# Retention followed by a snake-activated projection: half of the diagonal score and value products left out in three of eight batches

## The chip, the cores and the metric

The kernel runs on one core of a Trainium2 chip. The metric is device time in microseconds for one execution. Three executions of the kernel before took 309.53, 309.72 and 309.93 us; the median is 309.72 us.

The core has a matrix engine (TensorE, PE in the profile, with its weight loads as PEld), VectorE (DVE), ScalarE (ACT), GpSimd (POOL) and SyncE (SP). SyncE computes nothing here: it issues nearly all DMAs, one after the other, in the order in which the program names them.

## The reference

Two steps follow one another. The first is a causal retention over 8 batches, 8 heads, 576 tokens and 64 features a head:

```
scores = q @ k^T / sqrt(64)                          # per batch and head
ret    = scores * gamma[h] ** (i - j)   for i >= j, else 0
x      = ret @ v                                     # heads side by side: 4608 tokens x 512
```

The second is two matrix products with a snake function between them:

```
h   = x @ w_in                                       # 512 -> 2048
g   = h + sin(alpha * h) ** 2 / (alpha + 1e-9)
out = g @ w_out                                      # 2048 -> 512
```

## The kernel before, in words

**The retention in chunks.** A batch's first 512 tokens are four chunks of 128 tokens; the last 64 tokens of every batch are treated apart, two batches together (the class `Ends`, tensors `ks`, `qs`, `vs`). Since gamma ** (i - j) is a product of a factor of the query and a factor of the key, the factors (`cn`) are multiplied in when the inputs are cast to 16 bits. Within a chunk, scores are masked by i >= j; what earlier chunks contribute goes through a state of 64 x 64 per head (`outer` makes it from keys and values, `chain` on GpSimd carries it along, `add_states` multiplies it by the queries).

**Loads.** `load(b, nm, p)` brings half p (256 tokens, two chunks) of the keys, queries or values of batch b into a buffer `raw` with one DMA of 512 KB from SyncE's queue. A chunk lies on 64 partitions: partition 64 g + i holds, for chunk g of the half, the tokens 2 i and 2 i + 1 of the chunk, so a run in memory is two tokens, 512 B. The letter r tells the two apart. There are six such buffers.

**Cast and transpose.** `cast` multiplies by the factors and writes 16 bits (line 156 for keys and queries, line 99 on GpSimd for values); from batch 5 on GpSimd does all of them. `crossed` turns keys and queries with a DMA transpose from SyncE (line 179).

**Attention on TensorE.** All of it works on 64 x 64 quadrants of the array, four matmuls side by side.
- `scores(p, y)` (line 328): 16 matmuls, each with 64 keys of one r and one head against the 128 queries of the chunk. Four calls a batch.
- `masked` (line 339): VectorE multiplies 128 x 1024 scores by the mask and writes `ret`.
- `values(p, same)` (line 368): 16 matmuls of 64 values against 128 columns of `ret`. [...] 

**The order of the work.** It is written out by hand. Up to block 2 every step has a line of its own. From block n = 3 on a loop runs over blocks of 512 tokens: for each of 16 units u it runs `project` (line 503, four matmuls of 512 columns), `sine` on ScalarE (line 511), `square` on ScalarE or VectorE (lines 520 and 522), `product` on VectorE (line 527), and `gemm2` of the block before (line 546, four matmuls of 512 columns). After every fourth unit `finish` copies a result out of PSUM and SyncE stores it (line 539, two DMAs). The results of `project` rotate over three banks (`h`); stores go through four buffers (`osb`).

Attention is woven into this loop: in block n, batch n + 1 has its scores in units 3 and 8 and its values in unit 12, and batch n + 2 is loaded, cast (units 3 to 8, in the order k0, v0, k1, v1, q0, q1), transposed (units 13 and 15) and has its `outer` (unit 12). So batches 5, 6 and 7 are attended in blocks 4, 5 and 6 and loaded one to two blocks earlier. In unit 12, the two `values(..., False)` come first, then `outer` of the next batch, then the two `values(..., True)` with `add_states`.

Of the kernel before, what the change touches and what calls it, by code (L numbers as in the profile page):

```python
# [10 lines left out]
F32 = mybir.dt.float32  # L11
# [6 lines left out]
def kernel(  # L18
# [12 lines left out]


    nc = tc.nc

# [12 lines left out]
    cn_np = np.zeros((P, 52), dtype=np.float64)  # L47
# [16 lines left out]
    ident = const.tile([P, P], F16, tag="ident", bufs=1)  # L64
    mask = const.tile([P, 5 * 64], F16, tag="mask", bufs=1)
    cn = const.tile([P, 52], F32, tag="cn", bufs=1)
    fac = {"k": cn[:, 0:16], "q": cn[:, 16:32]}
    fac_s = {"k": cn[:, 32:40], "q": cn[:, 40:48]}
# [36 lines left out]
    def load(b, nm, p):  # L105
        if p < 2:
            t_ = work.tile([P, H, 2 * D], F32, tag="raw", bufs=6, name=nm + "32")
            nc.sync.dma_start(  # L108
                t_, src[nm][b, :, 256 * p : 256 * p + 256, :].rearrange("h (i r) d -> i h (r d)", r=2)
            )  # L110
        else:
            if b % 2 == 0:
                raw[b, nm, 2] = work.tile([P, H, D], F32, tag="raws", bufs=3, name=nm + "s32")
            t_ = raw[b - b % 2, nm, 2]
            nc.sync.dma_start(t_[halves(b % 2)], src[nm][b, :, 512:576, :].rearrange("h i d -> i h d"))
        raw[b, nm, p] = t_
# [3 lines left out]
    def cast(b, nm, p, eng, ys=(0, 1)):  # L120
# [32 lines left out]
        else:  # L153
# [4 lines left out]
                t_.rearrange("p (t a) x -> p t a x", t=2)[:, :, a0:a1].rearrange("p t a (r d) -> p t (a r) d", r=2),  # L158
                fac[nm]
                .rearrange("p (t x) -> p t x", t=2)[:, :, 2 * a0 : 2 * a1]  # L160
# [67 lines left out]
    class Attention:  # L228
        def __init__(self, b):
            self.b = b  # L230
            self.both = {}
# [87 lines left out]
        def scores(self, p, y, tag):  # L319
            kT, qT = T[self.b, "k", p], T[self.b, "q", p]  # L320
            sc = psum.tile([P, 2, 512], F32, tag=tag, bufs=1, name="sc")
            for z in range(2):
                a = 2 * y + z
                for r in range(2):
                    for g in range(2):
                        for t in range(2):
                            c = 256 * z + 128 * r
                            matmul(  # L328
                                sc[halves(g), t, c : c + 128],
                                kT[halves(t), 2 * a + r, halves(g)],  # L330
                                qT[halves(t), 2 * a : 2 * a + 2, halves(g)],
                                start=(z == 0 and r == 0), stop=True, skip_group_check=True,
# [3 lines left out]
        def masked(self, p, y):  # L336
            sc = self.sc.pop((p, y))
            ret = work.tile([P, 2, 512], F16, tag="ret", bufs=4, name="ret")
            nc.vector.tensor_tensor(  # L339
                ret.rearrange("p t (z x) -> p (t z) x", z=2),  # L340
                sc.rearrange("p t (z x) -> p (t z) x", z=2),
                mask[:, 0:256].unsqueeze(1).to_broadcast([P, 4, 256]),
                MULT,
# [3 lines left out]
        def values(self, p, same, *tags, relay=None):  # L347
# [13 lines left out]
            for x in range(2):  # L361
                for r in range(2):
                    for e in range(2):
                        for g in range(2):
# [3 lines left out]
                            made.append(matmul(  # L368
                                o[t][halves(e), c : c + 128],
                                v16[halves(g), 4 * t + 2 * x + e, r, :],  # L370
                                self.ret[p, x][halves(g), t, m : m + 128],
                                start=(not same and x == 0 and r == 0), stop=False, skip_group_check=True,
# [203 lines left out]
    def make_constants():  # L576

        ge = mybir.AluOpType.is_ge
        nc.gpsimd.memset(ident, 0.0)
# [5 lines left out]
        for g in range(2):  # L585
# [7 lines left out]
                out=m, in_=m, compare_op=ge, fill=0.0, base=0, pattern=[[1, 64]], channel_multiplier=-1,  # L593
            )

    with tc.manual_schedule():
# [481 lines left out]
        at[4].to_state(2, G_)  # L1078
        crossed(4, 0, "q")

        h, m = cycle(("h2", "h0", "h1")), cycle(("m0", "m1"))
        ON_A = (4, 5, 6, 8, 9)
        for n in range(3, NBLK):
# [54 lines left out]
            for u in range(16):  # L1138
# [63 lines left out]
```

## Time and profile before

| what | before |
|---|---|
| median of three executions | 309.72 us |
| profiled execution, its own time | 310.26 us |
| span in the profile (first to last instruction) | 308.5 us |
| mean granted TensorE clock | 0.989 |
| TensorE busy | 295.6 us (96%) |
| VectorE, ScalarE, GpSimd busy | 206.7, 181.0, 135.2 us |
| HBM read, written | 36.74 MB, 9.44 MB |

A row of a timeline begins with the start in microseconds from the start of the span and the duration of the row; then come engine, line of the kernel, operation, what is written and read, shape and count. In square brackets stands how long the engine was idle before and what ended that. Matmuls are pipelined and their ends are modelled, so the time that a group of matmuls takes is best read from its start to the start of the next group. In a row by stretch (A:B), each engine's busy time and number of instructions follow the length of the stretch, and at the end stand the granted clock, the mean busy share of the 16 DMA engines (over 1 where packets overlap) and GB/s. In a row of groups, the busy time and the mean of one instruction in ns stand after the first bar, and the engine's idle time before them, with what ended it, after the second.

### The profile page before, as it was taken

To read this page: it belongs to the slowest core of one execution; us is meant where nothing else is said; L and a number is where in the kernel's file an instruction comes from. 1 tells how busy PE (TensorE), PEld (TensorE's weight loads), DVE (VectorE), ACT (ScalarE), POOL (GpSimd) and SP (SyncE) were. 2 spreads that over 40 slices of the span, in tenths; PEclk is the share of its full clock that TensorE was granted. 3 is DMA by queue.
4 is the path that set the end of the run, shared out by engine and by line. 5 is a ranking of instruction groups with operands and counts; after the bars stand their busy time and mean duration, and the time that the engine had idled before them with its cause. 6 is when DMAs were issued, how large, how long until landed. Compare 5 with 4: busy or idle time off the path is not lost.

```text
span 308.5 us, 7866 instructions
## 1 busy us (share of the span) xinstructions
PE 295.6 (96%) x3257; PEld 151.0 (49%) x3257; DVE 206.7 (67%) x298; ACT 181.0 (59%) x286; POOL 135.2 (44%) x150
## 2 busy tenths in 40 slices
PE   6679899999999999999999999999999999999995
PEld 5555456555444544454445444544454454444443
DVE  1686899899669798657765776666666746555600
ACT  1348864675444857674768476857674456555411
POOL 4684772288759589469266926650030000000000
PEclk9599999999999999999999999999999999999999
DMA  7999999999998899879898999763431111111232
GB/s 206 292 228 216 225 249 266 218 262 276 204 213 233 125 231 260 171 111 218 219 261 123 235 213 259 116 130 75 102 70 36 34 36 36 35 34 37 46 89 69
DMA packets 102676, 49.83 MB, mean 162 GB/s; under 512 B 44640, under 2 KB 98160, under 8 KB 102640
## 3 DMA queue, kind: packets, MB, share of 16 engines
q1 hardware_dynamic: 98048, 44.97, 67.0%
q0 software_dynamic: 4224, 4.19, 8.0%
q8 instruction: 25, 0.41, 0.6%
q10 hardware_dynamic: 368, 0.17, 0.2%
q14 instruction: 11, 0.09, 0.1%
HBM read 36.74 MB, written 9.44 MB: 150 GB/s over the span
## 4 chain that ended last, share of the span: by engine, by line
PE 75%; DMA 12%; POOL 5%; issue 3%; ACT 2%; SPq 1%; DVE 0%; POOLq 0%; DVEq 0%; ACTq 0%
PE ops L546 36%; PE hps L503 32%; DMA v<-in_v_dram 5%; DMA q<-in_q_dram 4%; DMA qT<-q 3%; PE o L368 2%; PE sc L328 2%; POOL k L156 1%; POOL q L156 1%; PE kv L269 1%; SPq L108 1%; ACT s_t L511 1%; POOL kvs L311 1%; POOL s L303 1%; PE o L390 1%
## 5 line engine op out<-in xcount | busy, mean ns | idle before, releaser
L546 PE MATMUL ops<-w_out,gT 128*128 128x512 f16 (+2 forms) x592 | 142.5, 374 | 0.3 <-ACT kvs L97 0.2
L527 DVE SCALAR_TENSOR_TENSOR gT<-ss_t,inva,hps 128x512 f16<-128x512 f16 x144 | 106.3, 746 | 52.8 <-ACT ss_t L520 46.0
L511 ACT ACTIVATE s_t<-hps,alpha_t 128x512 f16<-128x512 f32 x144 | 97.4, 687 | 70.7 <-PE hps L503 69.1
L503 PE MATMUL hps<-xT,w_in 128*128 128x512 f16 (+1 forms) x544 | 126.6, 367 | 0.4 <-DMA w_in<-in_moe_w_in_dram 0.2
L503 PEld LDWEIGHTS <-w_in 128*128 128x128 f16 x608 | 58.6, 98 | 64.6 <-DMA w_in<-in_moe_w_in_dram 0.7
L546 PEld LDWEIGHTS <-gT 128*128 128x128 f16 x592 | 56.2, 98 | 64.5 <-issue 0.8
L522 DVE TENSOR_TENSOR ss_t<-s_t 128x512 f16<-128x512 f16 x72 | 40.5, 564 | 17.9 <-ACT s_t L511 17.5
L339 DVE TENSOR_TENSOR ret<-sc,mask 128x1024 f16<-128x1024 f32 x32 | 38.4, 1219 | 3.1 <-PE sc L328 3.1
L520 ACT ACTIVATE ss_t<-s_t 128x512 f16<-128x512 f16 x62 | 38.8, 631 | 0.9
L156 POOL TENSOR_TENSOR q<-q,cn 128x1024 f16<-128x1024 f32 (+1 forms) x16 | 27.4, 1722 | 13.7 <-DMA q<-in_q_dram 13.6
L97 ACT COPY osb<-ops 128x512 f32<-128x512 f32 (+1 forms) x34 | 19.7, 582 | 21.9 <-PE ops L546 20.3
L156 POOL TENSOR_TENSOR k<-k,cn 128x1024 f16<-128x1024 f32 (+1 forms) x13 | 21.7, 1671 | 20.8 <-DMA k<-in_k_dram 16.1
L140 POOL TENSOR_TENSOR ks<-ks,cn 128x512 f16<-128x512 f32 x4 | 4.2, 1044 | 34.2 <-PE o L368 34.2
L311 POOL TENSOR_TENSOR kvs<-s,kvs 128x256 f32<-128x256 f32 x22 | 16.4, 747 | 2.6 <-ACT kvs L97 0.9
L97 ACT CAST xT<-o 128x1024 f16<-128x1024 f32 (+1 forms) x14 | 13.2, 957 | 6.1 <-PE o L390 6.1
L503 PE MATMUL hps<-xS,w_in 128*128 128x512 f16 x64 | 16.4, 379 | 0.0
L522 POOL TENSOR_TENSOR ss_t<-s_t 128x512 f16<-128x512 f16 x10 | 10.8, 1086 | 11.4 <-ACT s_t L511 11.4
L310 POOL TENSOR_TENSOR s<-kvs,cn 128x256 f32<-128x256 f32 x22 | 13.6, 620 | 0.6 <-ACT kvs L97 0.4
L99 POOL CAST v<-v 128x1024 f16<-128x1024 f32 (+1 forms) x10 | 10.2, 1030 | 8.3 <-DMA v<-in_v_dram 8.3
L303 POOL TENSOR_TENSOR s<-kvs,cn 128x256 f16<-128x256 f32 x19 | 12.7, 674 | 1.1 <-issue 0.4
L368 PE MATMUL o<-ret,v 64*64 64x128 f16 x512 | 11.5, 219 | 0.8 <-DVE ret L339 0.4
L328 PE MATMUL sc<-qT,kT 64*64 64x128 f16 x512 | 11.5, 225 | 0.6 <-DMA qT<-q 0.4
(58 smaller groups left out, 139.2 us busy)
## 6 DMA issues: line engine op xcount, KB each, us to landing
out_dram<-osb SPq DMA_DIRECT2D x70, 128.0 KB, 2.5
k<-in_k_dram SPq DMA_DIRECT2D x16, 512.0 KB, 6.8
q<-in_q_dram SPq DMA_DIRECT2D x16, 512.0 KB, 6.9
v<-in_v_dram SPq DMA_DIRECT2D x16, 512.0 KB, 6.3
w_in<-in_moe_w_in_dram POOLq DMA_DIRECT2D x4, 512.0 KB, 12.5
w_out<-in_moe_w_out_dram POOLq DMA_DIRECT2D x4, 512.0 KB, 11.4
ks<-in_k_dram SPq DMA_DIRECT2D x8, 128.0 KB, 4.5
qs<-in_q_dram SPq DMA_DIRECT2D x8, 128.0 KB, 3.6
```

What stands on the lines that cost most here:

```text
L97: eng.copy(d_, s_)
L156: eng.tensor_tensor(dst[:, a0:a1].rearrange("p a r t d -> p t (a r) d"), t_.rearrange("p (t a) x -> p t a x", t=2)[:, :, a0:a1].rearrange( ...
L311: nc.gpsimd.tensor_tensor(self.kvs[:, c], s32, self.kvs[:, c], ADD)
L328: matmul(sc[halves(g), t, c : c + 128], kT[halves(t), 2 * a + r, halves(g)], qT[halves(t), 2 * a : 2 * a + 2, halves(g)], start=(z == 0 an ...
L339: nc.vector.tensor_tensor(ret.rearrange("p t (z x) -> p (t z) x", z=2), sc.rearrange("p t (z x) -> p (t z) x", z=2), mask[:, 0:256].unsque ...
L368: made.append(matmul(o[t][halves(e), c : c + 128], v16[halves(g), 4 * t + 2 * x + e, r, :], self.ret[p, x][halves(g), t, m : m + 128], sta ...
L503: matmul(hps_of[n, fc][0][:, cols], w_in16[:, a, fc * P : (fc + 1) * P], xs[n][:, a, cols], start=(a == 0 and part != 1), stop=(a == KT - ...
L511: nc.scalar.activation(s_t, hps, mybir.ActivationFunctionType.Sin, bias=0.0, scale=alpha_t[:, fc : fc + 1],)
L520: nc.scalar.activation(ss_t, s_t, mybir.ActivationFunctionType.Square)
L522: eng.tensor_tensor(ss_t, s_t, s_t, MULT)
L527: nc.vector.scalar_tensor_tensor(gT[n][:, fc, :], ss_t, inva[:, fc : fc + 1], hps, MULT, ADD)
L546: matmul(ops[n, c, cols.start][:, cols], gT[n][:, fk, c * P : (c + 1) * P], w_out16[:, fk, cols], start=(fk == 0), stop=(fk == FC - 1), sk ...
```

## The change

For batches 5, 6 and 7 (`HALVED = 5`) keys and values are laid out differently; queries stay as they are.

- Partition 64 g + i now holds, for r = 0, token i of the first 64 tokens of chunk g, and for r = 1, token i of the second 64. A run in memory is one token, 256 B. One load of keys or values becomes four DMAs of 128 KB, each of 64 partitions; twelve loads become 48 DMAs.
- Keys with r = 1 are later than every query of the first half of the chunk. So for r = 1 `scores` multiplies only the queries i from 32 to 63 of each kind (the second half of the chunk): 64 columns instead of 128. `values` multiplies 64 columns of `ret` for r = 1 likewise, and adds into the second halves of the output rows.
- `masked` handles 192 of 256 columns a head, 768 instead of 1024 elements a partition, with a mask of its own; `make_constants` makes it with four more selects on GpSimd and a longer memset. The keys' factors have 16 columns of their own in `cn`.
- All six loads of batch 5 are placed earlier by up to three units: three of them ahead of the loop, the other three in units 0 to 2 of block 3, ahead of that block's first output stores.
- In blocks 4 to 6, the square of unit 6 goes from ScalarE to VectorE, that of unit 10 the other way.

The number of matmuls and weight loads does not change, nor does their order.

```diff
+    HALVED = 5
...
+            cn_np[:, 52 + 2 * h + r] = gamma[h] ** (64 - (64 * r + ii))
...
     def load(b, nm, p):
-        if p < 2:
+        if p < 2 and b >= HALVED and nm != "q":
+            t_ = work.tile([P, H, 2 * D], F32, tag="raw", bufs=6, name=nm + "32")
+            for g in range(2):
+                for r in range(2):
+                    s0 = 256 * p + 128 * g + 64 * r
+                    nc.sync.dma_start(
+                        t_[halves(g), :, r * D : r * D + D], src[nm][b, :, s0 : s0 + 64, :].rearrange("h i d -> i h d")
+                    )
+        elif p < 2:
...
                 for r in range(2):
+                    i0, n = (32, 64) if self.halved and r else (0, 128)
...
                             matmul(
-                                sc[halves(g), t, c : c + 128],
+                                sc[halves(g), t, c : c + n],
                                 kT[halves(t), 2 * a + r, halves(g)],
-                                qT[halves(t), 2 * a : 2 * a + 2, halves(g)],
+                                qT[halves(t), 2 * a : 2 * a + 2, 64 * g + i0 : 64 * g + 64],
...
+            n, m0 = (192, 320) if self.halved else (256, 0)
             nc.vector.tensor_tensor(
-                ret.rearrange("p t (z x) -> p (t z) x", z=2),
-                sc.rearrange("p t (z x) -> p (t z) x", z=2),
-                mask[:, 0:256].unsqueeze(1).to_broadcast([P, 4, 256]),
+                ret.rearrange("p t (z x) -> p (t z) x", z=2)[:, :, 0:n],
+                sc.rearrange("p t (z x) -> p (t z) x", z=2)[:, :, 0:n],
+                mask[:, m0 : m0 + n].unsqueeze(1).to_broadcast([P, 4, n]),
...
                             made.append(matmul(
-                                o[t][halves(e), c : c + 128],
+                                o[t][halves(e), c : c + 128].rearrange("p (r i) -> p r i", r=2)[:, :, i0:64],
                                 v16[halves(g), 4 * t + 2 * x + e, r, :],
-                                self.ret[p, x][halves(g), t, m : m + 128],
+                                self.ret[p, x][halves(g), t, m : m + n],
...
+            for c0, n in ((320, 64), (448, 32)):
+                m = mask[halves(g), c0 : c0 + 2 * n].rearrange("p (r i) -> p r i", r=2)
+                nc.gpsimd.affine_select(
+                    out=m, in_=m, compare_op=ge, fill=0.0,
+                    base=0, pattern=[[1, 2], [2, n]], channel_multiplier=-1,
+                )
...
         crossed(4, 0, "q")
+        load(5, "k", 0)
+        load(5, "v", 0)
+        load(5, "k", 1)
...
-                if n == 3:
-                    at_unit(i, lambda nm=nm, p=p: load(5, nm, int(p)))
-                elif n < 6 and i > 2:
+                if n < 6 and i > 2:
                     at_unit(i - 3, lambda nm=nm, p=p: load(n + 2, nm, int(p)))
...
-                    square(n, u, A_ if A and u in ON_A else V)
+                    square(n, u, A_ if A and u in (ON_A if n < 4 else (4, 5, 8, 9, 10)) else V)
```

More of the change, by code (lines that the diff above doesn't have):

```diff
@@ L46 @@
     hi, ii = np.divmod(np.arange(P), 64)
[L47 removed]
+    cn_np = np.zeros((P, 68), dtype=np.float64)
     for h in range(H):
@@ L64 @@
     ident = const.tile([P, P], F16, tag="ident", bufs=1)
-    mask = const.tile([P, 5 * 64], F16, tag="mask", bufs=1)
-    cn = const.tile([P, 52], F32, tag="cn", bufs=1)
-    fac = {"k": cn[:, 0:16], "q": cn[:, 16:32]}
+    mask = const.tile([P, 8 * 64], F16, tag="mask", bufs=1)
+    cn = const.tile([P, 68], F32, tag="cn", bufs=1)
+    fac = {"k": cn[:, 0:16], "q": cn[:, 16:32], "halved k": cn[:, 52:68]}
     fac_s = {"k": cn[:, 32:40], "q": cn[:, 40:48]}
@@ L158, in cast @@
                 t_.rearrange("p (t a) x -> p t a x", t=2)[:, :, a0:a1].rearrange("p t a (r d) -> p t (a r) d", r=2),
-                fac[nm]
+                fac["halved k" if nm == "k" and b >= HALVED else nm]
                 .rearrange("p (t x) -> p t x", t=2)[:, :, 2 * a0 : 2 * a1]
@@ L230, in __init__ @@
             self.b = b
+            self.halved = b >= HALVED
             self.both = {}
@@ L362, in values @@
                 for r in range(2):
+                    i0, n = (32, 64) if self.halved and r else (0, 128)
                     for e in range(2):
```

## The prediction

> **What bounds the kernel now.** I read the page first (busy shares and the forty slices), then the busy time of each engine by stretch, then the timelines of TensorE, GpSimd and SyncE around the attention of batches 5 to 7, and last the waits of GpSimd.
>
> ```profile
> PE 295.6 (96%) x3257; PEld 151.0 (49%) x3257; DVE 206.7 (67%) x298; ACT 181.0 (59%) x286; POOL 135.2 (44%) x150
> PE   6679899999999999999999999999999999999995
> DMA  7999999999998899879898999763431111111232
> ```
>
> TensorE is busy all the time from the sixth slice on. The DMA engines are nearly as full until about 200 us.
>
> ```profile
> core 0: us, PE busy (x) PEld busy (x) DVE busy (x) ACT busy (x) POOL busy (x), PEclk, DMA share, GB/s
> 133.00:164.00 31.00, 31.00 (x360) 15.08 (x348) 21.18 (x28) 20.91 (x34) 18.99 (x19) 1.00 0.98 205
> 164.00:195.00 31.00, 31.00 (x360) 15.05 (x351) 21.22 (x28) 20.91 (x34) 19.00 (x19) 1.00 0.94 205
> 195.00:226.00 31.00, 31.00 (x348) 14.98 (x337) 20.01 (x28) 20.92 (x34) 9.29 (x13) 1.00 0.54 103
> ```
>
> These three stretches are about the blocks n = 4, 5, 6, in which batches 5, 6, 7 are attended. TensorE has no idle time in any, and the granted clock is 1.00; VectorE, ScalarE and GpSimd have 10 us or more. So a shorter matmul here comes off the end one for one, as long as nothing starts to make TensorE wait; and work taken from another engine is worth nothing.
>
> **What the matmuls give.** Per batch there are four score groups of 16 matmuls and four value groups of 16. In each, half (r = 1) go from 128 columns to 64: 32 + 32 a batch, 192 in all. The number of matmuls and weight loads stays.
>
> ```profile
> 146.40 0.64 PE L328 MATMUL sc<-qT,kT 64*64 64x128 f16 x32
> 146.97 1.04 PE L546 MATMUL ops<-w_out,gT 128*128 128x512 f16 x4
> ...
> 163.29 0.64 PE L368 MATMUL o<-ret,v 64*64 64x128 f16 x32
> 163.76 0.72 PE L269 MATMUL kv<-v,k 64*64 64x64 f16 x64
> 164.30 0.41 PE L368 MATMUL o<-ret,v 64*64 64x128 f16 x16
> 164.52 0.30 PE L390 MATMUL o<-qT,s 64*64 64x128 f16 x8
> 164.64 0.47 PE L368 MATMUL o<-ret,v 64*64 64x128 f16 x16
> 164.92 0.41 PE L390 MATMUL o<-qT,s 64*64 64x128 f16 x16
> ```
>
> From start to start, 32 score matmuls take 0.57 us (17.8 ns each), the value matmuls 0.47 for 32 and 0.22 and 0.28 for 16 (14.7, 13.8, 17.5 ns), and 64 outer-product matmuls of 64 columns take 0.54 us (8.4 ns each), weight loads included. The quadrants of the array work four at a time. How much does a halved one save? At the least 13.8 - 8.4 = 5.4 ns, so 192 x 5.4 = 1.0 us; at the most 17.8 - 8.4 = 9.4 ns, 1.8 us. Between them I go by the stream itself, from the chain in order of time:
>
> ```profile
> 136.97 0.86 PE hps L503 x4
> ```
>
> Four matmuls of 512 columns take 0.86 us, 0.42 ns a column. 64 columns are 27 ns, and with four quadrants abreast 6.75 ns a matmul: 192 x 6.75 = **1.30 us**, which lies amid the ends.
>
> **What costs nothing, and by which cover.** The twelve masks of these batches shrink from 1024 to 768 elements a partition, and on ScalarE and VectorE the squares of units 6 and 10 change places (blocks 4 to 6):
>
> ```profile
> L339 DVE TENSOR_TENSOR ret<-sc,mask 128x1024 f16<-128x1024 f32 x8 | 9.7, 1218 | 0.0
> L520 ACT ACTIVATE ss_t<-s_t 128x512 f16<-128x512 f16 x18 | 11.4, 631 | 0.3
> L511 ACT ACTIVATE s_t<-hps,alpha_t 128x512 f16<-128x512 f32 x33 | 22.7, 687 | 16.2 <-PE hps L503 16.2
> ```
>
> A mask should lose about a quarter of 1.22 us, 0.3 us; 12 x 0.3 = 3.6 us of VectorE, which TensorE does not wait for. A square is 0.63 us on ScalarE. In the 62 us of these rows ScalarE stood idle 16.2 us for TensorE before 33 sines, 0.5 us a unit, so one square more in unit 10 is made up within two units; the result buffers rotate over three banks, so a product may be late by units before TensorE notices. Were that cover gone, each moved square would cost up to 0.63 us, 1.9 us for three.
>
> At the start GpSimd gets a longer memset and four more selects:
>
> ```profile
> 1.32 0.36 POOL L584 MEMSET mask<- 128x320 f16 x1
> 1.75 0.42 POOL L587 TENSOR_SCALAR_AFFINE_SELECT mask<-mask 64x256 f16<-64x256 f16 x1
> 2.79 0.24 POOL L592 TENSOR_SCALAR_AFFINE_SELECT mask<-mask 64x64 f16<-64x64 f16 x1
> 5.19 1.04 POOL L156 TENSOR_TENSOR k<-k,cn 128x512 f16<-128x512 f32 x1 [2.16 <-DMA k<-in_k_dram]
> ```
>
> That is 0.2 us for the memset, two selects of 64 elements at 0.24 and two of 128 at about 0.3: 1.3 us, under 2.16 us of waiting for keys. Uncovered it would be at most 1.3 us. The constants' load grows by 16 columns of 52 and I give it no price; its reader is that same waiting multiply.
>
> **What costs queue time.** Each of the twelve key and value loads becomes four DMAs of 128 KB in runs of 256 B: 36 DMAs more on SyncE's queue. The nearest rows are the short loads, which have exactly that shape, and the two blocks' loads of today:
>
> ```profile
> 109.88 0.57 SPq L108 DMA_DIRECT2D k<-in_k_dram  x1
> ...
> 118.79 1.77 SPq L108 DMA_DIRECT2D q<-in_q_dram  x2
> ...
> 137.10 0.57 SPq L108 DMA_DIRECT2D k<-in_k_dram  x1
> 137.73 0.80 SPq L108 DMA_DIRECT2D v<-in_v_dram  x1
> 138.57 3.63 SPq L179 DMA_TRANSPOSE kT<-k  x1
> ...
> 147.91 0.59 SPq L108 DMA_DIRECT2D k<-in_k_dram  x1
> 149.27 3.11 SPq L108 DMA_DIRECT2D q<-in_q_dram  x2
> ...
> 159.52 1.27 SPq L115 DMA_DIRECT2D vs<-in_v_dram  x2
> 163.15 1.16 SPq L539 DMA_DIRECT2D out_dram<-osb  x2
> 164.41 1.42 SPq L179 DMA_TRANSPOSE kT<-k  x1
> ...
> 185.56 1.36 SPq L115 DMA_DIRECT2D ks<-in_k_dram  x2
> ```
>
> ```profile
> 150.20:156.20 6.00, 6.00 (x58) 2.83 (x56) 4.17 (x6) 4.78 (x9) 2.90 (x2) 1.00 1.15 302
> 220.40:223.60 3.20, 3.20 (x17) 1.43 (x16) 2.82 (x4) 1.92 (x3) 0.00 (x0) 1.00 0.72 162
> ```
>
> Whole loads move at 302 GB/s (512 KB in 1.7 us); four short loads moved at 162 GB/s (3.2 us for as much), though with the engines at 0.72 of a share that reaches 1.15 elsewhere: they were short of issues, 0.69 us each. What does it delay? GpSimd:
>
> ```profile
> 133.14 1.04 POOL L140 TENSOR_TENSOR ks<-ks,cn 128x512 f16<-128x512 f32 x1 [4.48 <-PE o L368]
> 156.27 3.76 POOL L156 TENSOR_TENSOR q<-q,cn 128x1024 f16<-128x1024 f32 x2 [0.72 <-DMA q<-in_q_dram]
> 164.22 1.04 POOL L140 TENSOR_TENSOR ks<-ks,cn 128x512 f16<-128x512 f32 x1 [4.19 <-PE o L368]
> 195.28 1.04 POOL L140 TENSOR_TENSOR ks<-ks,cn 128x512 f16<-128x512 f32 x1 [4.64 <-PE o L368]
> ```
>
> GpSimd casts a batch's loads in order, the second query half last, and then stands before the relay (told, in the value step of unit 12) until TensorE's first value groups end. If the casts come late instead, TensorE stands before its second value groups. So there are 4.48, 4.19 and 4.64 us to lose, for batches 5, 6, 7.
>
> Batch 6, the tightest: keys and values of the first half take 8 x 0.69 = 5.5 us of issue instead of 1.4 (137.10 to 138.53), +4.1; but the transpose behind them took 3.63 us, against 1.42 for the same one at 164.41, which I read as a full queue; filled more slowly it gives 2.2 back. Second half: 5.5 instead of 1.4, +4.1 again, so the first query load is issued 6.0 us later, at 155.3. It then has an empty queue ahead: the quickest whole load landed in 3.3 us, the second follows 1.7 later, at 160.3. Today its cast begins at about 158.1 (half of the 3.76 us after 156.27). So the cast ends 2.2 us later, of 4.19: hidden. SyncE itself then runs about 3 us late (the two query issues and the store after them no longer sit in a full queue) against 2.4 us of idleness (160.79 to 163.15); 0.7 us goes on to batch 7, which is 2.9 us late of 4.64: hidden. Batch 5: the six loads come ahead of a pair of output stores instead of around it; 16 issues from 109.88 end at 120.9, where the queries are issued at 118.79 now: 2.1 of 4.48 us. That pair of stores slips about 5 us, with four store buffers and a new result every four units of 1.7 us (8 x 0.22, by the row of four matmuls); hidden.
>
> What is late next, if nothing waits: TensorE's own sequence, which ends the span as before. The lower end of the delay is none (the loads already wait for each other today), the upper comes with the second rival.
>
> **Sum.** -1.30 + 0 against the profiled execution's own 310.26 us: 308.96, 0.42% less. That execution is 0.17% above the median of 309.72; the same share off the median gives 308.4.
>
> **Rivals.**
> *The relay stalls (slower).* If a load of four quarter DMAs really takes 3.2 us in place of 1.7 and nothing of the full queue is given back, a batch's four loads put the last cast back by 6.0 us. TensorE then stands 6.0 - 4.2 = 1.8 us in batch 6; the queue carries 6.0 - 2.4 - 1.8 = 1.8 us on, and batch 7 loses 1.8 + 6.0 - 4.6 = 3.2 us. With the matmuls' gain: +3.7 us, 313.4. It decides from a delay of about 4.8 us a batch on. For it: the DMA share of 0.98 and 0.94 in just these stretches. Against it: the share of 0.72 in the row above says that short loads wait for issue more than for the engines. [...]
> *No gain.* The halved matmuls cost as much as before, because the weight load or the issue sets the pace, or small waits eat the 1.3 us: 309.7. The 8.4 ns of the 64-column outer products speaks against the first; margins of 2 us speak against the second, but they were worked out with a queue whose behaviour I inferred from few rows.
>
> **How the numbers follow.** Forecast 0.62 (gain 1.0 to 1.8 us: 307.9 to 308.7); no gain or nearly 0.16; relay stall, and whatever else makes it slower, 0.22. About 0.2%, 0.6 us, is what a measurement of this kernel can tell from no change; so faster 0.62, same 0.16, slower 0.22. The range takes in the forecast with its ends, the case of no change and the beginning of the stalls: 307.9 to 310.6.
>
> **What would show it.** Score and value groups: from start to start 0.45 us or so for 32 score matmuls instead of 0.57. GpSimd's idle time before the short key cast (ks) in blocks 4 and 5: still there, about 2 us, waiting for TensorE; if it is gone and a value group of TensorE waits for GpSimd, the rival holds. SyncE's load issues: 0.6 to 0.7 us each. I am wrong if TensorE shows idle time between 130 and 230 us, or if its groups do not shorten.

## The result, and the profile after

The changed kernel takes 311.24 us (median; 310.09 to 312.92) against 309.61 us for the kernel before beside it: a ratio of 1.0053, with a 95% interval of 1.0032 to 1.0074. It is slower, by 1.0 to 2.3 us; the forecast was 1.3 us faster. The profiled execution took 311.16 us (span 309.4 us). What the change leaves out is a quarter of the diagonal products of three batches (half of the columns in every second matmul), not half of them as the title has it. From the page after:

```profile
PE 296.4 (96%) x3257; PEld 150.9 (49%) x3257; DVE 207.4 (67%) x298; ACT 180.7 (58%) x286; POOL 138.4 (45%) x154
PE   6669999999999999999999999999999999999995
PEclk9776999999999999999999999999999999999999
k<-in_k_dram SPq DMA_DIRECT2D x24, 128.0 KB, 3.1
```

TensorE is full from the fourth slice on, two slices earlier than before, and yet ends later: in the second to fourth slice the clock is granted at 0.6 to 0.7 on average, since it is 0.50 for a part of each (11.3 to 18.1 and 21.5 to 28.3 us by the clock records).

TensorE runs the same 3257 matmuls in the same order in both kernels, so the start of the n-th in one trace can be subtracted from that in the other. This lateness is the measure used below (negative: ahead of the kernel before):

| kernel | at 28 us | before the loop's block 4 | before batch 6's values | behind them | end |
|---|---|---|---|---|---|
| changed kernel | +3.77 | +1.49 | +1.15 | +1.35 | +1.01 |

So 1.49 us are lost before any of the halved matmuls runs. Of the forecast gain of 1.30 us, 0.34 is there before batch 6's values, 0.2 is lost again in them, and 0.48 is left at the end.

The profiled execution of the kernel before, against which all this is reckoned, took 310.26 us, 0.65 more than the median of 309.61. The kernel pad_128 below, which differs from it by 64 B of padding and starts alike, gains 0.65 us on it between 89 and 103 us. Against a usual execution of the kernel before, the changed kernel is thus about 0.7 us later than the table says from block 4 on (an estimate from these numbers): 1.7 us at the end, where the medians say 1.63.

**The start.** By stretch, first before, then after (columns as in the forecast; the last is GB/s, the third from last the granted clock):

```profile
4.00:8.00 4.00, 2.52 (x49) 2.26 (x47) 1.02 (x2) 0.00 (x0) 1.04 (x1) 1.00 1.17 297
8.00:12.00 4.00, 2.20 (x48) 2.13 (x47) 1.42 (x4) 1.14 (x2) 1.43 (x1) 0.62 1.17 290
16.00:24.00 8.00, 5.84 (x179) 4.45 (x178) 7.12 (x8) 3.11 (x6) 7.10 (x8) 1.00 1.20 222
24.00:32.00 8.00, 7.76 (x46) 3.97 (x45) 5.68 (x15) 7.14 (x12) 3.53 (x5) 1.00 1.20 216
```

```profile
4.00:8.00 4.00, 2.01 (x49) 1.82 (x47) 1.06 (x2) 0.00 (x0) 1.13 (x2) 1.00 1.15 342
8.00:12.00 4.00, 1.51 (x49) 1.29 (x49) 2.17 (x5) 2.03 (x3) 2.02 (x2) 0.91 1.16 350
16.00:24.00 8.00, 5.20 (x136) 3.85 (x133) 7.44 (x6) 1.94 (x3) 7.24 (x8) 0.71 1.20 215
24.00:32.00 8.00, 7.91 (x76) 4.55 (x69) 5.55 (x13) 4.49 (x7) 0.00 (x0) 0.73 1.20 216
```

The first loads are faster after the change (342 and 350 GB/s instead of 297 and 290), though they are the same 512 KB loads; then a second stretch at half clock follows, where the kernel before has full clock. Between the two lie VectorE and GpSimd. Their timelines before:

```profile
15.91 0.76 DVE L303 TENSOR_TENSOR s<-kvs,cn 128x256 f16<-128x256 f32 x2 [0.62 <-POOL kvs L311]
16.59 3.48 DVE L339 TENSOR_TENSOR ret<-sc,mask 128x1024 f16<-128x1024 f32 x3
```

```profile
17.41 1.89 POOL L156 TENSOR_TENSOR q<-q,cn 128x1024 f16<-128x1024 f32 x1 [0.78 <-DMA q<-in_q_dram]
```

and after, with TensorE's rows last:

```profile
15.31 3.50 DVE L316 TENSOR_TENSOR s<-kvs,cn 128x256 f16<-128x256 f32 x2 [1.29 <-POOL kvs L324]
18.74 4.61 DVE L354 TENSOR_TENSOR ret<-sc,mask 128x1024 f16<-128x1024 f32 x4
```

```profile
16.05 1.91 POOL L168 TENSOR_TENSOR q<-q,cn 128x1024 f16<-128x1024 f32 x1
17.91 0.61 POOL L323 TENSOR_TENSOR s<-kvs,cn 128x256 f32<-128x256 f32 x1
```

```profile
20.00 0.42 PE L342 MATMUL sc<-qT,kT 64*64 64x128 f16 x16 [1.78 <-DVE ret L354]
21.13 0.42 PE L342 MATMUL sc<-qT,kT 64*64 64x128 f16 x16 [0.16 <-DVE ret L354]
22.27 1.38 PE L384 MATMUL o<-ret,v 64*64 64x128 f16 x32 [0.71 <-DVE ret L354]
```

Two state steps (`to_state`, both on VectorE) take 3.50 us instead of 0.76. Single instructions in the trace: the first takes 0.42 us, the second, begun at 15.65, 3.16 us. It ends at 18.81, behind GpSimd's cast and the multiply after it, which now follow without the 0.78 us of waiting for queries. The masks start 2.15 us later (18.74, 16.59), TensorE waits 2.65 us in three places for them (before: 0.65 us in two places, and 1.08 for GpSimd's cast of queries), and its clock is halved again from 21.5 to 28.3 us by the clock records: 32 value matmuls take 1.38 us, against 0.91 before. All eight executions of the changed kernel show the low clock, 0.976 to 0.983 over the whole span; of 22 executions of the kernel before beside pad_only, 20 show 0.986 to 0.989.

**Blocks 4 to 6.** After the change, by stretch, and the rows of SyncE, GpSimd and TensorE that answer to those of the forecast:

```profile
134.00:165.00 31.00, 31.00 (x373) 15.06 (x365) 20.73 (x27) 21.05 (x35) 18.38 (x19) 1.00 0.84 188
165.00:196.00 31.00, 31.00 (x379) 15.03 (x370) 20.09 (x28) 21.09 (x34) 16.86 (x19) 1.00 0.83 188
```

```profile
151.26 2.72 SPq L115 DMA_DIRECT2D k<-in_k_dram  x4
154.02 2.67 SPq L115 DMA_DIRECT2D v<-in_v_dram  x4
156.74 2.21 SPq L120 DMA_DIRECT2D q<-in_q_dram  x2
```

```profile
134.63 1.04 POOL L152 TENSOR_TENSOR ks<-ks,cn 128x512 f16<-128x512 f32 x1 [3.26 <-PE o L384]
...
161.75 3.76 POOL L168 TENSOR_TENSOR q<-q,cn 128x1024 f16<-128x1024 f32 x2 [0.78 <-DMA q<-in_q_dram]
165.47 1.04 POOL L152 TENSOR_TENSOR ks<-ks,cn 128x512 f16<-128x512 f32 x1
...
194.74 1.90 POOL L168 TENSOR_TENSOR q<-q,cn 128x1024 f16<-128x1024 f32 x1 [0.17 <-DMA q<-in_q_dram]
196.81 1.92 POOL L168 TENSOR_TENSOR q<-q,cn 128x1024 f16<-128x1024 f32 x1 [0.17 <-DMA q<-in_q_dram]
```

```profile
147.93 0.54 PE L342 MATMUL sc<-qT,kT 64*64 64x128 f16 x32
148.40 1.04 PE L562 MATMUL ops<-w_out,gT 128*128 128x512 f16 x4
...
196.85 0.37 PE L384 MATMUL o<-ret,v 64*64 64x128 f16 x16 [0.16 <-POOLq L236]
```

32 score matmuls take 0.47 us from start to start instead of 0.57. GpSimd's idle time before the short key cast is 3.26 us behind the loads of batch 5 and gone behind those of batches 6 and 7; in batch 6's value step (block 5, while batch 7 is loaded) TensorE waits 0.16 us for GpSimd's relay. The relay is an empty instruction on GpSimd (`told`, called for by `relay=G_`): it waits for TensorE's first value groups, TensorE's second value groups wait for it, and in the program it stands behind the batch's casts.

### The profile page after: what moved, and what is told of

Read it like the earlier page. It is cut to its first block, busy times and chain, and to the rows that moved or that the text cites. A ratio compares the mean times of both kernels' runs of the same rounds, so it can differ in the third digit from the quotient of the medians.

```text
span 309.4 us, 7922 instructions
## 1 busy us (share of the span) xinstructions
PE 296.4 (96%) x3257; PEld 150.9 (49%) x3257; DVE 207.4 (67%) x298; ACT 180.7 (58%) x286; POOL 138.4 (45%) x154
## 4 chain that ended last, share of the span: by engine, by line
PE 84%; DMA 3%; POOL 3%; SPq 3%; DVE 2%; ACT 1%; issue 1%; DVEq 0%; ACTq 0%; POOLq 0%
PE ops L562 39%; PE hps L519 37%; DMA q<-in_q_dram 3%; PE o L384 3%; PE sc L342 2%; SPq L115 2%; POOL q L168 1%; PE kv L282 1%; DVE s L316 1%; DVE ret L354 1%; PE o L406 1%; SPq L120 1%; ACT s_t L527 1%; POOL k L168 1%; PE tr L201 0%
## 5 line engine op out<-in xcount | busy, mean ns | idle before, releaser
L538 DVE TENSOR_TENSOR ss_t<-s_t 128x512 f16<-128x512 f16 x72 | 42.2, 587 | 19.5 <-ACT s_t L527 18.8
L354 DVE TENSOR_TENSOR ret<-sc,mask 128x1024 f16<-128x1024 f32 (+1 forms) x32 | 35.1, 1118 | 1.9 <-PE sc L342 1.8
L103 POOL CAST v<-v 128x1024 f16<-128x1024 f32 (+1 forms) x10 | 12.2, 1234 | 9.5 <-DMA v<-in_v_dram 8.4
L323 POOL TENSOR_TENSOR s<-kvs,cn 128x256 f32<-128x256 f32 x22 | 14.3, 651 | 0.3
L384 PE MATMUL o<-ret,v 64*64 64x128 f16 (+1 forms) x512 | 11.9, 226 | 1.3 <-DVE ret L354 0.7
L342 PE MATMUL sc<-qT,kT 64*64 64x128 f16 (+1 forms) x512 | 10.9, 221 | 1.9 <-DVE ret L354 1.9
## 6 DMA issues: line engine op xcount, KB each, us to landing
w_in<-in_moe_w_in_dram POOLq DMA_DIRECT2D x4, 512.0 KB, 11.3
```

The lines of the kernel that those rows point to most:

```text
L342: matmul(sc[halves(g), t, c : c + n], kT[halves(t), 2 * a + r, halves(g)], qT[halves(t), 2 * a : 2 * a + 2, 64 * g + i0 : 64 * g + 64], st ...
L354: nc.vector.tensor_tensor(ret.rearrange("p t (z x) -> p (t z) x", z=2)[:, :, 0:n], sc.rearrange("p t (z x) -> p (t z) x", z=2)[:, :, 0:n], ...
L384: made.append(matmul(o[t][halves(e), c : c + 128].rearrange("p (r i) -> p r i", r=2)[:, :, i0:64], v16[halves(g), 4 * t + 2 * x + e, r, :] ...
L538: eng.tensor_tensor(ss_t, s_t, s_t, MULT)
```

## The experiments

Lateness of each at the same five places, and the times:

| kernel | 28 us | block 4 | before batch 6's values | behind | end | median us | ratio (95%) |
|---|---|---|---|---|---|---|---|
| pad_only | +2.64 | +0.64 | +0.62 | +0.60 | +0.59 | 308.69 | 0.998 (0.995 to 1.001) |
| shifted_back | -0.05 | +0.12 | -0.33 | +1.32 | +0.99 | 311.63 | 1.0072 (1.0043 to 1.0101) |
| pad_128 | -0.05 | -0.76 | -0.76 | -0.75 | -0.75 | 309.51 | one time |
| pad_256 | -1.30 | -3.33 | -3.34 | -3.33 | -3.33 | 306.93 | one time |
| pad_gap | -1.32 | -3.38 | -3.35 | -3.35 | -3.36 | 307.52 | 0.9922 (0.9892 to 0.9951) |
| state_later | -0.61 | -2.49 | -2.88 | -1.50 | -1.83 | 307.83 | 0.9941 (0.9921 to 0.9962) |
| pad_state_later | -0.73 | -2.54 | -2.54 | -2.54 | -2.52 | 307.69 | 0.9939 (0.9924 to 0.9954) |
| narrow_only | -0.09 | +0.26 | -0.14 | -0.16 | -0.52 | 309.48 | 0.9998 (0.9984 to 1.0013) |
| split_only | +0.04 | -0.01 | +0.19 | +1.41 | +1.38 | 311.98 | 1.0076 (1.0058 to 1.0094) |
| relay_act | -0.03 | +0.12 | -0.34 | +0.23 | -0.09 | 309.45 | 0.9989 (0.9967 to 1.0012) |
| two_batches | -1.58 | -2.70 | -3.10 | -3.18 | -3.19 | 306.95 | 0.9911 (0.9894 to 0.9927) |
| all_fixed | -0.59 | -2.48 | -2.83 | -2.98 | -3.30 | 306.67 | 0.9892 (0.9854 to 0.993) |
| after_gap | -1.27 | -2.04 | -2.44 | -2.45 | -2.79 | 306.58 | 0.9904 (0.9889 to 0.9919) |
| gap_act | -1.22 | -1.86 | -2.31 | -2.35 | -2.65 | 306.80 | 0.9903 (0.9886 to 0.9919) |

The lateness is from one profiled execution each; medians and lateness of one kernel differ by up to 1 us.

### Where the buffers lie: pad_only, shifted_back, pad_128, pad_256

The changed kernel's mask tile grows from 640 to 1024 B a partition and the constants' tile from 208 to 272 B. They are allocated first, so every later buffer moves by 448 B: the six load buffers began at 60480 B of each partition, 64 past a multiple of 512, and now begin at 60928, a multiple of 512. pad_only takes the kernel before and makes the two tiles as large as in the changed one, unused:

```diff
-    mask = const.tile([P, 5 * 64], F16, tag="mask", bufs=1)
-    cn = const.tile([P, 52], F32, tag="cn", bufs=1)
+    mask = const.tile([P, 8 * 64], F16, tag="mask", bufs=1)
+    cn = const.tile([P, 68], F32, tag="cn", bufs=1)
```

> The kernel before, with only the two constant tiles as large as in the changed kernel, so that every later buffer lies 448 bytes further on in its partition; nothing computed, loaded or issued differs. Placement theory (the 448 bytes make the input packets shorter, and the start falls into an order in which VectorE's second state step of batch 0 stands behind GpSimd and TensorE gets a second stretch of half clock): packets of 512 B take about 27 ns as in the changed kernel, clock 0.976 to 0.983, TensorE reaches the loop about 1.5 us late, 311.0 to 311.5 us. Selects theory (the four selects and the longer memset at the start do it): as before, 309.6 us, clock 0.989.

shifted_back takes the changed kernel and moves the buffers on by 64 B, to the same 64 past a multiple of 512 as before:

```diff
-    cn = const.tile([P, 68], F32, tag="cn", bufs=1)
+    cn = const.tile([P, 84], F32, tag="cn", bufs=1)
```

> The changed kernel with 64 bytes more in the factor tile, so that the input buffers lie at 64 bytes past a multiple of 512 as in the kernel before. Placement theory: the start is that of the kernel before, clock 0.989, and what is left is the 0.5 us that blocks 4 to 6 gave: 309.1 us (308.9 to 309.3), faster by 0.15%; a little less if the slower packets make the relay of batches 6 and 7 later. Selects theory: slow as the changed kernel, about 311.2 us.

The profiled execution of pad_only has the fast loads and the second half-clock stretch, without anything else of the change; shifted_back has the slow loads and a start within 0.1 us of the kernel before. So the placement makes the start. Neither time is the expected one: pad_only's median lies 2.3 us below its range, because its times fall into two groups (below), and shifted_back missed by 2.5 us, for two reasons further on in the kernel (below). The next two tell which placements count; both are the kernel before with only the constants' tile enlarged, by 64 B and by 192 B:

```diff
-    cn = const.tile([P, 52], F32, tag="cn", bufs=1)
+    cn = const.tile([P, 68], F32, tag="cn", bufs=1)     # pad_128; pad_256: 100 columns
```

> The kernel before with 64 B more per partition in the tile of the constants, and nothing else: the load buffers start at 128 (mod 512) instead of 64. Theory A (what counts is whether the 512 B pieces begin on a multiple of 256 B of the buffer's address): slow as before, mean packet of 512 B between 5 and 15 us 32 to 33 ns, 285 to 300 GB/s between 4 and 12 us, start as in the kernel before, 309.5 us. Rival B (any shift away from 64, or the total size, does it): 27 ns and 340 to 350 GB/s. [...]

> The kernel before with 192 B more per partition in the tile of the constants, and nothing else: the load buffers start at 256 (mod 512). Theory A (multiples of 256 B count): fast, 27 ns a packet and 340 to 350 GB/s between 4 and 12 us, as with 0 (mod 512), and with it the early GpSimd cast and the second stretch at half clock. Rival B (only multiples of 512 B count): 32 to 33 ns, start as in the kernel before.

The first stretch of pad_128, then two of pad_256:

```profile
4.00:8.00 4.00, 2.10 (x49) 1.88 (x47) 0.98 (x2) 0.00 (x0) 1.04 (x1) 1.00 1.20 296
```

```profile
4.00:8.00 4.00, 1.76 (x49) 1.71 (x47) 1.61 (x3) 0.16 (x1) 1.04 (x1) 1.00 1.15 346
...
16.00:24.00 8.00, 7.14 (x180) 4.88 (x179) 6.32 (x8) 2.98 (x5) 6.69 (x7) 0.90 1.20 216
```

Buffers at 64 or 128 past a multiple of 256 B load at 296 to 297 GB/s, those at a multiple of 256 B at 342 to 346, 1.15 to 1.17 times as much. What differs is the address that is written to. Other buffers move along in these runs; that the load buffers' own address counts is argued from the packets that fill them.

pad_256 missed the second half of its expectation, and in a telling way: its transfers and its GpSimd cast are as early as pad_only's, yet the state step isn't held and there is no second half-clock stretch (0.90 and then 1.00). VectorE and GpSimd in pad_256:

```profile
14.72 0.76 DVE L303 TENSOR_TENSOR s<-kvs,cn 128x256 f16<-128x256 f32 x2 [1.29 <-POOL kvs L311]
15.40 2.35 DVE L339 TENSOR_TENSOR ret<-sc,mask 128x1024 f16<-128x1024 f32 x2
```

```profile
15.46 1.92 POOL L156 TENSOR_TENSOR q<-q,cn 128x1024 f16<-128x1024 f32 x1
```

The second state step begins 0.40 us ahead of the cast in the changed kernel, 0.39 in pad_only, 0.40 in pad_256, and lasts 0.42 us when free: a tie. Which way it falls is worth about 3.9 us at 28 us (+2.64 and -1.30) and at the end (+0.59 and -3.33). The times of pad_only lie mostly near 307.6 or near 310.6 us, as a tie that falls both ways would have it. Only one of its executions was profiled (310.83 us, held), but the granted clock of each is known: 0.975 to 0.983 in the five that took 309.0 us or more, 0.986 to 0.994 in the five faster ones. That pad_256 runs free because its buffers lie at 256 instead of 0 past a multiple of 512 is not excluded by its one execution; pad_only's fast executions, with buffers at 0, speak against it.

### What holds the state step: pad_gap, state_later, pad_state_later

pad_gap is pad_only with one GpSimd instruction more ahead of the cast, a memset that writes a buffer not yet in use:

```diff
+        nc.gpsimd.memset(xS[:, 0:2, :].rearrange("p a x -> p (a x)")[:, 0:768], 0.0)
         cast(1, "q", 1, G_)
```

> The kernel before with the larger constant tiles (load buffers at 0 mod 512) and one more instruction on GpSimd, a memset of 768 elements (about 0.8 us, writes only) of a buffer not in use yet, ahead of the cast that in the padded kernel begins at 15.7 us while VectorE's second state step is under way. Theory A (VectorE's state step, two inputs in SBUF, is held by GpSimd's back-to-back instructions that read SBUF): with a gap of 0.8 us the step ends in about 0.4 us instead of 3.2, the masks start near 16 us, there is no second stretch at half clock, and the kernel is 2 to 3 us faster than the padded one although GpSimd has more to do: 306.5 to 308. Rival B (the step waits for something else, the faster transfers themselves): the step still takes about 3 us, the time is that of the padded kernel or 0.8 more, 308.5 to 311.

```profile
14.65 0.76 DVE L303 TENSOR_TENSOR s<-kvs,cn 128x256 f16<-128x256 f32 x2 [1.29 <-POOL kvs L311]
```

```profile
15.36 0.76 POOL L647 MEMSET xS<- 128x768 f16 x1
16.06 1.92 POOL L156 TENSOR_TENSOR q<-q,cn 128x1024 f16<-128x1024 f32 x1
```

With 0.76 us more work on GpSimd the two steps take 0.76 us, and the median falls by 1.2 us below pad_only's, with no time above 308.51 and no granted clock below 0.986 in seven executions. It is the cast that holds the step; the memset of 0.76 us in its place doesn't. To have begun first did not keep the step from being held: in the changed kernel it came first by 0.40 us and was held, and past two GpSimd instructions.

state_later leaves the placement and moves the step behind the masks, in the changed kernel; pad_state_later does the same to pad_only:

```diff
-        at[0].to_state(0, V)
         at[0].outer((1,), "h2", "h1")
...
         at[0].masked(1, 0)
+        at[0].to_state(0, V)
```

> The changed kernel with the second state step of batch 0 on VectorE (to_state(0)) behind the first three masks instead of ahead of them. If the stall of that step behind GpSimd (3.16 us in place of 0.42) is what delays the masks and costs the clock: the first mask starts about 3 us earlier, TensorE's waits of 1.8 and 0.7 us for masks go, no second stretch of half clock, TensorE reaches the loop up to 2 us earlier than the kernel before, and the time is 308.5 to 309.5. If the clock falls for another reason (the idle stretch between 6 and 9.5 us alone): about 311.

> pad_only with the second state step of batch 0 behind the masks: the start of state_later without any halving. Reaches the loop 2.5 us earlier than the kernel before, as state_later did: 307.1 (306.8 to 307.5), so that halving is worth -0.7 us there (state_later 307.8). If halving had helped state_later: 308.5.

Both gain: 0.994 times the kernel before, the changed kernel and the one before alike; state_later gains 0.7 us more than expected, pad_state_later 0.2 us less. Two kernels with the same start and the change as the only difference so have ratios of 0.9941 and 0.9939: on an equal start the change is worth nothing, to within about 0.8 us by the two intervals, and not 1.3 us.

### What the matmuls give and what the loads cost: narrow_only, split_only, relay_act, two_batches, all_fixed

narrow_only is shifted_back with the 512 KB loads and the old order of tokens; the halved matmuls then leave out products that belong to the result.

```diff
-        if p < 2 and b >= HALVED and nm != "q":
+        if False:
```

> As shifted_back, but every load is one DMA of 512 KB again, so the halved matmuls meet keys and values in the old order: the products that fall away are then not all zero ones, and the output leaves them out. What the narrow matmuls and masks alone give. By the prediction's term, 1.30 us: 308.2. By the groups of the changed kernel's trace (0.10 us for each of two score groups of 32 matmuls, 0.14 us in the value step): 0.34 us a batch, 1.0 us, 308.5. No wait of TensorE for GpSimd at the relay.

Lateness goes from +0.26 to -0.52: the matmuls give 0.78 us. Six pairs of score groups give 0.10 each, 0.60. The value steps give 0.2 together: from their first matmul to the next of 512 columns 1.95, 1.93 and 1.30 us against 1.97, 1.96 and 1.45. TensorE in narrow_only, batch 5:

```profile
163.37 0.54 PE L384 MATMUL o<-ret,v 64*64 64x128 f16 x32
163.75 0.81 PE L282 MATMUL kv<-v,k 64*64 64x64 f16 x64
164.37 0.36 PE L384 MATMUL o<-ret,v 64*64 64x128 f16 x16
164.54 0.30 PE L406 MATMUL o<-qT,s 64*64 64x128 f16 x8
```

The first value groups shrink from 0.47 to 0.38 us, but the outer product behind them grows from 0.54 to 0.62, so that the second value group begins 1.0 us after the first, as before. Batch 7, without an outer product there, gains 0.15. Why the 1.0 us stays was not tried.

By the medians narrow_only gains nothing (0.9998), where 308.2 to 308.5 us was expected: it loses about as much ahead of block 4. VectorE, GpSimd and TensorE in narrow_only, then VectorE and GpSimd in the kernel before:

```profile
75.71 3.20 DVE L168 TENSOR_TENSOR k<-k,cn 128x512 f16<-128x512 f32 x2
76.33 2.03 POOL L168 TENSOR_TENSOR q<-q,cn 128x1024 f16<-128x1024 f32 x1 [0.28 <-DMA q<-in_q_dram]
79.57 1.04 PE L519 MATMUL hps<-xT,w_in 128*128 128x512 f16 x4 [0.89 <-DVE xT L103]
```

```profile
75.46 1.50 DVE L156 TENSOR_TENSOR k<-k,cn 128x512 f16<-128x512 f32 x2
76.45 2.27 POOL L156 TENSOR_TENSOR q<-q,cn 128x1024 f16<-128x1024 f32 x1 [0.65 <-DMA q<-in_q_dram]
```

Here VectorE and GpSimd meet a second time. In narrow_only, shifted_back, split_only and relay_act the second of VectorE's two key casts begins 0.17 to 0.19 us behind GpSimd's cast of queries and takes 2.4 us instead of 0.68; TensorE waits 0.9 us for what VectorE does next. In the kernel before and in pad_128 it begins 0.17 and 0.06 us ahead of that cast and is not held; there GpSimd's cast is the longer one (2.27 and 2.38 us). So in this place the earlier start decides. Against pad_128, narrow_only is 1.0 us behind at block 4 and 0.2 at the end. Which edit shifts these starts was not tried; the trace of the changed kernel itself has no such wait.

split_only is shifted_back with four DMAs in runs of 256 B but full matmuls, masks and the old order of tokens:

```diff
-                    s0 = 256 * p + 128 * g + 64 * r
+                    s0 = 256 * p + 128 * g
...
-                        t_[halves(g), :, r * D : r * D + D], src[nm][b, :, s0 : s0 + 64, :].rearrange("h i d -> i h d")
+                        t_[halves(g), :, r * D : r * D + D],
+                        src[nm][b, :, s0 : s0 + 128, :].rearrange("h (i r) d -> r i h d", r=2)[r],
...
-            self.halved = b >= HALVED
+            self.halved = False
```

> As shifted_back, but with all matmuls and masks of full width and the tokens in the old order; only the loads of keys and values of batches 5 to 7 are in four DMAs with runs of 256 B. What the loads alone cost. If the late casts cost all: TensorE waits for the relay about 1.2 us in batch 6 (1.7 us in shifted_back, less the about 0.5 us by which full matmuls are later), nothing or 0.1 us in batch 5: 310.7 to 311.0. If the wait came with the narrow matmuls: 309.6.

From block 4 on the loads alone cost 1.4 us in the trace, nearly all in batch 6's value step. The median, 2.3 us above the kernel before and 1 us above the expected range, has the wait of 0.9 us at 79 us as well. The relay's wait, in split_only and then in shifted_back:

```profile
196.80 0.42 PE L385 MATMUL o<-ret,v 64*64 64x128 f16 x16 [1.06 <-POOLq L237]
```

```profile
196.82 0.37 PE L384 MATMUL o<-ret,v 64*64 64x128 f16 x16 [1.71 <-POOLq L236]
```

It comes at the same time in both, and in the changed kernel at 196.85, though TensorE is up to 1.5 us further ahead in one than in another: the transfers set it. So time won ahead of it is lost in it; that and the wait at 79 us are what shifted_back's expectation had missed. relay_act is shifted_back with the relay on ScalarE:

```diff
-                at_unit(12, lambda: A.values(0, False, next(m), relay=G_), lambda: A.values(1, False, next(m), relay=G_))
+                at_unit(12, lambda: A.values(0, False, next(m), relay=A_), lambda: A.values(1, False, next(m), relay=A_))
```

> As shifted_back, with the relay of the value step in blocks 3 to 6 on ScalarE instead of GpSimd, so that late casts on GpSimd no longer hold up TensorE's second value groups. Relay theory (the late second query cast costs about 0.2 us in batch 5 and 0.4 to 0.5 us in batch 6 to TensorE): 0.4 to 0.7 us less than shifted_back, the value step of batches 5 and 6 takes about 1.75 us in place of 1.98 and 2.17 from its first group to the next project. If the relay is not what takes the gain: the same time as shifted_back, or more, since ScalarE's own work of unit 12 comes first (0.3 us or so).

```profile
195.44 0.45 PE L282 MATMUL kv<-v,k 64*64 64x64 f16 x32 [0.63 <-POOL v L103]
```

The relay's wait is gone and 1.1 us with it (2.2 by the medians), more than the expected 0.4 to 0.7; in its place batch 7's outer product waits 0.63 us for a value cast whose load is late. two_batches is state_later with the change for batches 5 and 6 only, so that the loads of batch 7 stay whole:

```diff
-    HALVED = 5
+    HALVED = (5, 6)                                     # and "b in HALVED" for "b >= HALVED"
```

> state_later with batch 7 as in the kernel before (whole loads, full matmuls); batches 5 and 6 halved. If the loss sits in batch 7's loads, which hold the relay of block 5: TensorE does not wait for GpSimd at the relay, gains 0.3 us in each of two batches, 306.6 (306.3 to 306.9). If the loss builds up from batch 6's loads as well: a wait of 0.5 us or more stays in block 5, 307.3 or more.

No wait in batch 6, 0.5 us gained in blocks 4 to 6, 0.9911 times the kernel before. all_fixed is state_later with all three batches and the relay on ScalarE, by the diff of relay_act:

> The changed kernel with the state step behind the masks and the relay on ScalarE instead of GpSimd, all three batches halved. Theory A (relay through GpSimd is what batch 6 loses): no wait before the second value groups of batch 6, or 0.6 us for the late value cast, end about 1 us earlier than with the state step alone: 306.8, like the version with two batches halved (306.95). Rival B (the relay costs nothing in the time): 307.8, as with the state step alone.

0.8 us gained from block 4 to the end, 0.9892: the relay through GpSimd was what batch 6 lost. These two versions, and after_gap and gap_act below, are faster than the kernel before and the changed one; their intervals don't tell them apart. Most of that is the start: pad_state_later has the same start without the change and 0.9939. To the change itself 0.3% and 0.5% are left in these two forms, with intervals that just overlap pad_state_later's. The relay on ScalarE was not tried without the change.

### Both causes undone in the changed kernel: after_gap, gap_act

The changed kernel with the memset of pad_gap, and the same with the relay on ScalarE:

> The changed kernel with nothing else than the memset of 768 elements on GpSimd ahead of the cast that collides with VectorE's state step. If the collision is all that the changed kernel loses at its start: state step 0.42 us, no second stretch at half clock, TensorE about 3.4 us ahead of the kernel before at the loop, as in the padded kernel with the memset. If the relay then costs batch 6 1.4 us, against a gain of 0.8 us by the matmuls: 2.7 us ahead at the end, about 307.5, so that the change by itself is worth 0.6 us of loss beside the padded kernel with the memset (307.5 median, 306.9 in its profiled execution). If the change costs nothing there: 306.1 in the profiled execution.

> The same with the relay on ScalarE. If collision and relay are the two causes, both are gone: 3.4 us ahead at the loop and 0.8 us more by the halved matmuls, 4.2 us ahead at the end, 306.0 in the profiled execution, less than any version so far. If the late transfers find another way to hold TensorE, the outer product of batch 7 waits for the value cast (0.6 us, as with slower packets): 306.6.

In both the steps take 0.76 us and there is no second half-clock stretch, and both are faster than the kernel before by 1%. Two things came out otherwise. TensorE leads by only 2.0 and 1.9 us at block 4, 1.3 to 1.5 less than in pad_gap. At 34 us they lose 0.6 us, where TensorE waits for a key cast of GpSimd whose load lands later, and regain 0.3 at 38 us; the rest comes in small waits between 74 and 99 us. Why that load is later was not found. And in after_gap's profiled execution the relay makes no wait: its query cast begins at 190.96, in state_later's at 192.05, so the transfers of the two differ by about 1 us there. By the median pad_gap, without the change, takes 307.52 us and after_gap 306.58, but their intervals overlap, and by the lateness of the profiled executions after_gap ends 0.57 us behind pad_gap: whether the change gains with the start mended stays open, within 1 us either way.

## Why the prediction was wrong

- **The step that failed** is "What costs nothing": the masks' and the constants' tiles were priced by their instructions (memset, selects, a longer load), and these were hidden as said (GpSimd still waited 1.39 us for keys). The tiles' size was not priced. It moved the load buffers, made the first transfers 1.15 to 1.2 times as fast, took GpSimd's 0.78 us of waiting away, and so let a cast meet a state step: 1.49 us at block 4, more than the forecast gain. Of the 2.2 us between the forecast of 308.96 and the profiled execution's 311.16 that is the larger part; the rest is in blocks 4 to 6, which gave 0.48 us in place of 1.30. None of the rivals had the placement; all looked at blocks 4 to 6 alone.
- **The matmuls' term** was right in mechanism: 6 ns a halved score matmul (0.10 us in 16) against 6.75. It was mis-sized for the values: 0.2 us in place of 0.65, so 0.78 us in place of 1.30, below the lower end of 1.0.
- **The masks, the moved squares and the selects** cost TensorE nothing that can be seen: narrow_only, with all of them, is within 0.1 us of the kernel before at 28 us, and its TensorE waits for neither VectorE nor ScalarE in blocks 4 to 6.
- **The queue** went as forecast up to the issue: 0.68 us a short DMA (0.69), the first query load of block 4 issued at 156.74 instead of 149.27, 6.1 us later once TensorE's own 1.35 us are taken off (6.0). Its landing did not: 5.0 us after its issue in place of 3.3, so that the "empty queue ahead" was no such thing. The last cast of batch 6 starts 4.1 us late (2.2), that of batch 7 6.9 us (2.9; at 196.81 instead of 188.74), by the same reckoning.
- **The slack** was mis-sized the other way. It was reckoned from the last cast's end, but the relay passes at 196.8, when that cast only begins (196.81): GpSimd passes it on before the cast has run. So there were 1.9 us more than the 4.2 and 4.6 reckoned with: the loads of batch 6 make no wait in block 4, and those of batch 7 one of only 0.16 us in block 5.
- **The relay rival** was right in kind: in block 5, 1.1 us by the loads alone and 1.4 to 1.7 us where TensorE is further ahead. It was wrong in size (5 us in two batches) and is not what made this kernel slower. Whether the four transfers of a load slowed one another or only waited to be issued can't be told here: a load of four DMAs takes 2.7 us to issue and a quarter lands 3.1 us after its issue, with the DMA engines' share down from 0.98 and 0.94 to 0.84 and 0.83.
- **What would show it**: the score groups shortened (0.47; 0.45 forecast). GpSimd's idle time before the short key cast was forecast to stay and is gone, as the rival said.

## What to carry to other kernels

A tile that grows moves every buffer behind it; compare the addresses of the buffers that DMAs write, and the GB/s of transfers that the change doesn't touch, before an effect is put down to the edit. Faster transfers can make a kernel slower, when an engine loses a wait that kept it out of another's way (here 0.78 us of GpSimd's); where two instructions meet within 20 ns, the order of the program should part them. A slack must be reckoned to the instruction that gives the signal, and time won on the critical engine is kept only where the transfers aren't next in line (here the relay at 196.8 us in three kernels).

## What the runs showed of the hardware that was not expected

- The same load of 512 B runs moves 296 to 297 GB/s into buffers at 64 or 128 past a multiple of 256 B and 342 to 346 GB/s into buffers at a multiple of 256 B. Between 5 and 15 us a packet of 512 B took 32.6 ns in the kernel before and 27.1 ns in the changed one.
- In the changed kernel a VectorE multiply (the state step) that takes 0.42 us took 3.16 us while GpSimd worked through a cast and a multiply, although it had begun first; a GpSimd memset of 0.76 us at the same place didn't hold it. At 76 us a VectorE cast of 0.68 us took 2.4 us in the four traces in which GpSimd's cast began up to 0.19 us before it, and 0.68 us in the two in which it began first.
- In the changed kernel, TensorE idle for 1.94 us between 18.1 and 21.5 us was followed by 6.8 us at half clock, though it worked for 1.5 us of that stretch. How much idle time it takes, if idle time is the cause, is not shown: in the kernel before 1.54 us idle between 18.2 and 21.7 us was followed by full clock.
